# Moving loads ahead of stores at the start of the last part, a limit on how early operations begin, and joined final stores, in an attention + MoE kernel

## The chip, the cores and the metric

The kernel runs on one core of one Trainium2 chip. The metric is device time in microseconds (us) of one execution. One execution of the kernel before was profiled; three more were timed. All times of rows are microseconds from the start of the profiled span.

## What is computed

```python
attn_out = _attn_ref(q, k, v)          # 4 x 8 heads x 576 x 64
x = attn_out.transpose(0, 2, 1, 3).reshape(B * S, H * D)   # 2304 x 512
P = exp(x @ w_gate - max)              # 2304 x 8, then 8 rounds of row and column normalising
for e in range(8):
    h = np.maximum(x @ w1[e], 0.0)     # 512 -> 1024
    out += P[:, e:e + 1] * (h @ w2[e]) # 1024 -> 512
```

The attention is a sum of a coarse attention (over averages of four rows) and a local one. The last part, which the change is about, holds only MoE work: `h`, `h @ w2`, the gates and the sum over the experts, for the last third of the rows.

## The kernel before

Matrix products are made in fp32 precision out of three passes: each operand is split into a high part (`hi`, rounded, on ACT) and a low part (`lo`, the rest, on POOL or DVE), and hi·hi, hi·lo and lo·hi are added in PSUM. One product of a 256 x 512 block therefore is 6 matmuls of 512 columns.

The rows are cut in six chunks. The attention runs first, with MoE work of early chunks beside it; then comes a part in plain tiles and in blocks for chunks 0 to 3 (`blocks_part`, `plain_part` from line 2537); the **last part** (class `Plan`, `final_plan` at line 171, class `Final`) does chunks 4 and 5, `side_c` and `side_d`, for all 8 experts. It uses seven block products in the place of eight (the additions of blocks are on POOL for the weights and on DVE for the results). There are 16 steps, one for each expert and half of the hidden layer. A step has 14 products of the first layer (`l1`, matmuls of line 478, parts a and b) and 14 of the second (`l2`, line 490), 168 matmuls in all. A step's second layer runs between the products of the next step's first layer (`MID`); the first step begins with a first layer alone (`PRO`: a1 a2 a6 a5 b1 b2 a7 a4 a3 b6 b5 b7 b4 b3), and the last ends with `TAIL`, which also transposes the four sums back (`x11`, `x22`, `x12`, `x21`, line 528), copies them out of PSUM (line 537 on DVE, line 497 on ACT) and stores them (`x_store`, line 539).

The order of the last part's instructions on each engine is written by a list scheduler, `Plan.schedule` (line 95). Each operation has a cost and a due time, counted back from the matmuls that need it; each engine in turn takes, of what is ready, the operation with the earliest due time, as early as its inputs and buffers allow. The result is `work`, a list in the order of planned starts. The engines execute their own instructions strictly in that order, so an instruction that waits holds up all that stand behind it on the same engine.

The operations that matter here are:

- Weight loads (`w_load`, lines 440 and 445), issued by SP. A step has four blocks of 256 KB for each layer. First-layer blocks (ring `r1`, 7 buffers; they appear as `xh` and `xl`) take two DMAs of 128 KB, second-layer blocks (ring `r2`, 7 buffers, `r` and `r2x`) one. `r2x` is the seventh buffer of `r2` and lies in the pool `accc`, in memory that is free only after `few.close()`, when the sums of the part before have been stored.
- Gate loads (`g_load`, line 467; `ring g`, 3 buffers): 256 KB that spread one expert's gates over all partitions. Their buffers were used before by `t_gen`, whose last operations are those of line 2397.
- Conversions of weights: `hi` on ACT (line 457), `lo` on POOL (line 461), sums of blocks on POOL (line 448). Copies of PSUM into SBUF on ACT (line 497, `s`, `u`).

The last part begins inside the part before. `plain_part` has 8 steps, numbered -8 to -1 in `ahead`. At steps -3, -2 and -1 the operations are emitted whose planned start lies before the step's end; all others follow after the last step:

```python
            if i >= -3:
                while work and work[0].start < lead + (i + 1) * period_:
                    work.pop(0).emit()
```

In step -1, ahead of this, `closed` (line 2342) stores the four finished tiles of chunks 1 and 2: 16 DMAs of 64 KB on SP (line 2346), which wait for DVE's last sums (line 2363). By the plan, the four first-layer loads of the first step and the first gate load stand before these stores; the second gate load, all second-layer loads and the loads of the second step stand behind them.

At the end, `x_store` stores each of the eight 128 x 512 result tiles with four DMAs of 64 KB, all on SP: 32 in all.

Of the kernel before, what the change touches and what calls it, by code (L numbers as in the profile page):

```python
# [18 lines left out]
HOP_US = 0.06  # L19


class Op:
    def __init__(self, name, eng, iss, lat, deps, port, emit):
        self.name, self.eng, self.iss, self.lat, self.deps = name, eng, iss, lat, deps
        self.port, self.emit, self.users, self.vals, self.due = port, emit, [], [], None
        self.start = self.end = None
# [10 lines left out]
class Plan:  # L37
# [54 lines left out]
    def dma(self, name, kb, reads, writes, emit=None):  # L92
        return self.op(name, "sp", kb / 190.0, 2.2 + kb / 190.0, reads, writes, emit)

    def schedule(self, begin=None):
        begin = begin or {}
        t = begin.get("pe", 0.0)
        for o in self.seq:
            o.due = t
            t += o.iss  # L100
        for a, b in zip(self.seq, self.seq[1:]):
            if a not in b.deps:
                b.deps.append(a)
        vals = {}
        for o in self.ops:
            for v in o.vals:
                vals[id(v)] = v
        for v in vals.values():
            for o in v.new if v.before else ():
                o.deps += [d for d in v.before.all if d not in o.deps]  # L110
        for o in self.ops:
            for d in o.deps:
                d.users.append(o)
        left, topo = {id(o): len(o.deps) for o in self.ops}, [o for o in self.ops if not o.deps]
        for o in topo:
            for u in o.users:
                left[id(u)] -= 1
                if not left[id(u)]:
                    topo.append(u)
        assert len(topo) == len(self.ops)  # L120
        for o in reversed(topo):
            if o.eng != "pe":
                o.due = min(
                    [u.due - (o.iss if u.eng == o.eng else o.lat + HOP_US) for u in o.users], default=t + 1.0
                )
        clk = {e: begin.get(e, 0.0) for e in ("pe", "dve", "act", "pool", "sp")}
        clk["port"] = 0.0
        left = {id(o): len(o.deps) for o in self.ops}
        ready = {e: [] for e in clk}
        at = {}  # L130

        def release(o):
            at[id(o)] = max(
                [d.start + d.iss if d.eng == o.eng else d.end + HOP_US for d in o.deps], default=0.0
            )
            ready[o.eng].append(o)

        for o in self.ops:
            if not o.deps:
                release(o)  # L140
        done = []
        while len(done) < len(self.ops):
            best = None
            for e, l in ready.items():
                if not l:
                    continue
                z = [(max(at[id(o)], clk[e], clk["port"] if o.port else 0.0), o) for o in l]
                m = min(q[0] for q in z) + 0.05
                st, o = min((q for q in z if q[0] <= m), key=lambda q: q[1].due)
                if best is None or st < best[0]:  # L150
                    best = st, o
            st, o = best
            o.start, o.end = st, st + o.lat
            clk[o.eng] = st + o.iss
            if o.port:
                clk["port"] = st + o.iss
            ready[o.eng].remove(o)
            done.append(o)
            for u in o.users:
                left[id(u)] -= 1  # L160
                if not left[id(u)]:
                    release(u)
        return done
# [173 lines left out]
class Final:  # L337
# [1 line left out]

    TYPES = ("B11", "B21", "B22", "T1", "T2", "T3", "T4")  # L340

    def __init__(self, nc, pools, dram, x01, x, xt, sides, xq, w1, w2, lg, tbase, ident, out_rows):
        self.nc, self.pools, self.x01, self.xt, self.sides, self.xq = nc, pools, x01, xt, sides, xq
        self.lg, self.tbase, self.ident, self.out_rows = lg, tbase, ident, out_rows
        self.gd = dram.tile([8, 8, 128], F32, name="gd")
        self.w1 = w1.rearrange("e (k p) (h a i c) -> e p h i a k c", p=128, h=2, a=2, i=2)
        self.w2 = w2.rearrange("e (h a k p) (i c) -> e p h k i a c", p=128, h=2, a=2, i=2)
        self.made = {}
        (ah, bh_), (al, bl_) = ([z[c] for c in sides] for z in x)
        top, bot = slice(0, 2), slice(2, 4)  # L350
        self.x_op = {"B11": (ah[:, top], al[:, top]), "B21": (ah[:, bot], al[:, bot]), "B22": (bh_[:, bot], bl_[:, bot])}
        for i in range(4):
            s = slice(2 * i, 2 * i + 2)
            self.x_op[f"T{i + 1}"] = xt[0][:, s], xt[1][:, s]
        self.b_top = [z[:, k] for z in (bh_, bl_) for k in range(2)]
        self.pages_h = None
# [181 lines left out]

    def x_store(self, blk, j, o):
        i, c = int(blk[0]) - 1, self.sides[int(blk[1]) - 1]  # L540
        t_ = self.get(o[0])
        for t in range(2):
            for p0, m, dst in self.out_rows(c, 2 * j + t):
                self.nc.sync.dma_start(
                    out=dst[:, 256 * i:256 * i + 256], in_=t_[p0:p0 + m, 256 * t:256 * t + 256]
                )


@with_exitstack
def attention_moe_kernel(  # L550
# [10 lines left out]
    nc = tc.nc  # L561
# [4 lines left out]
    R = 4  # L566
# [11 lines left out]
    chunks = [(64 * i, 64) for i in range(3)] + [(192 + 128 * i, 128) for i in range(3)]  # L578
    NC = len(chunks)
    ntile = [R * n // 128 for _, n in chunks]  # L580
    tbase = [sum(ntile[:c]) for c in range(NC)]
# [11 lines left out]
    dram = ctx.enter_context(tc.tile_pool(name="dram", bufs=1, space=bass.MemoryType.DRAM))  # L593
# [9 lines left out]
    ident = const.tile([128, 128], F32, name="ident")  # L603
    lg = const.tile([128, NTILE, E], F32, name="lg")
# [4 lines left out]
    xh, xl = [None] * NC, [None] * NC  # L609
    xq_of = []  # L610
    x01 = []
# [31 lines left out]
    def mask_of(c):  # L643
        i = edged.index(c)
        return mask[:, i * 2 * R * W:(i + 1) * 2 * R * W]
# [65 lines left out]
    class Slot:  # L711
        def __init__(self):
            self.busy = False
            self.t = 0.0
# [1387 lines left out]
    def out_rows(c, t):  # L2102
# [3 lines left out]
        k_ = 128 // m  # L2106
        return [(m * i, m, rows[k_ * t + i, t0 // 2:t0 // 2 + m, :]) for i in range(k_)]

    with tc.manual_schedule():

        ini_ctx = ExitStack()
# [42 lines left out]
        for big in (True, False):  # L2154
            if big:
                fold(64)
            else:
                for o in (32, 96):
                    nc.vector.tensor_scalar(
                        out=eff[o:o + 32], in0=eff[o:o + 32], scalar1=-float(WR * 32), scalar2=None, op0=ALU.add  # L2160
                    )
            for c in edged:
                if is_small(c) == big:
                    continue
                t0, n = chunks[c]
# [4 lines left out]
                dst = mask_of(c)  # L2170
                nc.vector.tensor_scalar(
                    out=dst, in0=eff, scalar1=z + 0.5, scalar2=NEG, op0=ALU.is_le, op1=ALU.mult
                )
                nc.vector.scalar_tensor_tensor(
                    out=dst, in0=eff, scalar=a - 0.5, in1=dst, op0=ALU.is_ge, op1=ALU.mult
# [57 lines left out]
        begin = {"pe": 36.6, "dve": 38.2, "act": 39.0, "pool": 42.3, "port": 38.2, "sp": 42.0, "dma": 48.0}  # L2233
# [39 lines left out]
        n = m_end[0] // NF * NF  # L2273
# [5 lines left out]
        side_f, side_b, side_c, side_d = (1, 2), (3,), (4,), (5,)  # L2279
# [38 lines left out]
        th4 = cx.tile([128, 2 * KD, NS * 2], F32R, name="th4")  # L2318
        tl4 = cx.tile([128, 2 * KD, NS * 2], F32R, name="tl4")
# [447 lines left out]
        if both:  # L2767
# [10 lines left out]
            blocks_part(side_f, side_b, both, hf_a, hf_b, accp, g1, plain1, reload)  # L2778
        final = Final(
            nc, dict(wa=wa, wb=wb, ct=ct, hp=hp, rawp=rawp, ps_h=ps_h, ps_a=ps_a, ps_y=ps_y, ps_z=ps_z), dram,  # L2780
            x01, (xh, xl), (th4, tl4), (side_c[0], side_d[0]), xq_of[0], moe_w1, moe_w2, lg, tbase, ident, out_rows,
        )
        plan = final_plan(E * NH, final)
        lead = 12.0
        work = plan.schedule({"pe": lead})
        period_ = 5.45

        def ahead(i):
            if i == -8:
                final.gates()  # L2790
            if i >= -3:
                while work and work[0].start < lead + (i + 1) * period_:
                    work.pop(0).emit()

        plain_part(rest2, n + n1, len(units), t_gen(side_c, side_d, True), ahead)
        while nb[1] < len(back):
            back_add()
# [35 lines left out]
```

## Time and profile before

| | us |
|---|---|
| profiled execution | 1611.02 |
| its span (first to last instruction) | 1609.2 |
| three timed runs | 1611.98, 1614.25, 1614.31 (median 1614.25) |

The span holds all but 1.8 us of the profiled execution. In the slices, each digit is the busy share of a fortieth of the span in tenths; PEclk is the granted TensorE clock. In the timeline, a row is start, duration, engine, line and operation; in brackets stands the idle time of the engine ahead of it and what ended it. SPq and ACTq are the sequencers that issue DMAs.

### The profile page before, as it was taken

The numbers are of one execution on the slowest core, as the hardware profiler recorded it, in microseconds if no ns is written. First come the engines' busy times: TensorE is split into PE (matmuls) and PEld (weight loads), VectorE is DVE, ScalarE is ACT, GpSimd is POOL, SyncE is SP. The second block draws the span as 40 slices with busy tenths as digits, with TensorE's granted clock in tenths as the row PEclk, the third lists the DMA queues.
The fourth block names the chain that finished last, engine by engine and source line by source line (L and its number), as shares of the span: only waits on it lengthen the run. The fifth ranks groups of instructions, "written<-read, shape, count | busy, mean of one in ns | idle before, by whom it ended". The sixth has DMA issues, their size and how long they took to land.

```text
span 1609.2 us, 23207 instructions
## 1 busy us (share of the span) xinstructions
PE 1573.5 (98%) x7776; PEld 1308.5 (81%) x7776; DVE 1269.2 (79%) x1694; ACT 766.1 (48%) x1625; POOL 1018.9 (63%) x932
## 2 busy tenths in 40 slices
PE   9999999999999999999999997999999999999996
PEld 7888888888888788888888875788888888888885
DVE  8779998878888696477444465989999999999995
ACT  4553555465545443333333334555555555555542
POOL 6698666868495300455544245887888788887760
PEclk9999999999999999999999998999999999999998
DMA  8877767868684545354111433212222212121102
GB/s 202 212 212 208 166 164 183 209 184 220 146 230 125 154 141 178 90 152 118 53 52 50 127 90 102 72 53 73 63 75 58 80 54 66 53 66 53 46 14 53
DMA packets 224454, 186.96 MB, mean 116 GB/s; under 512 B 26126, under 2 KB 181966, under 8 KB 224078
## 3 DMA queue, kind: packets, MB, share of 16 engines
q1 hardware_dynamic: 218382, 174.72, 40.2%
q10 hardware_dynamic: 5952, 10.75, 1.9%
q8 instruction: 61, 1.00, 0.3%
q14 instruction: 59, 0.48, 0.1%
HBM read 165.33 MB, written 20.09 MB: 115 GB/s over the span
## 4 chain that ended last, share of the span: by engine, by line
PE 88%; DVE 5%; DMA 2%; SPq 2%; POOL 1%; issue 1%; ACT 1%; ACTq 0%; POOLq 0%; DVEq 0%
PE psm L490 17%; PE psm L478 17%; PE psh L1847 16%; PE psm L2596 7%; PE psy L1875 5%; PE psy L1876 5%; PE psy L1877 5%; PE psy L2678 3%; PE psy L2676 3%; PE psy L2677 3%; PE psh L2078 1%; DMA r<-in_moe_w_dram 1%; SPq L841 1%; DVE psm L500 1%; PE pss L1472 1%
## 5 line engine op out<-in xcount | busy, mean ns | idle before, releaser
L1996 POOL TENSOR_TENSOR w1l<-r,w1h 128x512 fp32r<-128x512 f32 x112 | 158.1, 1412 | 81.9 <-ACT w1h L1973 73.1
L478 PE MATMUL psm<-th,o 128*128 128x512 f32 x512 | 174.6, 392 | 13.1 <-ACT s L497 13.1
L1996 POOL TENSOR_TENSOR w2l<-r,w2h 128x512 fp32r<-128x512 f32 x114 | 155.6, 1365 | 28.7 <-ACT w2h L1973 28.4
L1875 PE MATMUL psy<-w2h,hh 128*128 128x512 f32 x416 | 168.6, 405 | 0.0
L1876 PE MATMUL psy<-w2l,hh 128*128 128x512 f32 x416 | 162.6, 391 | 0.0
L1877 PE MATMUL psy<-w2h,hl 128*128 128x512 f32 x416 | 162.5, 391 | 0.0
L461 POOL TENSOR_TENSOR o<-r,o 128x512 fp32r<-128x512 f32 x84 | 114.4, 1362 | 75.1 <-ACT o L457 59.9
L500 DVE TENSOR_TENSOR acc<-psm,acc 128x512 f32<-128x512 f32 x216 | 143.7, 681 | 18.3 <-PE psm L490 18.2
L490 PE MATMUL psm<-hx,o 128*128 128x512 f32 x576 | 154.4, 390 | 0.6 <-DVE hx L515 0.6
L1904 ACT ACTIVATE hh<-psh 128x512 fp32r<-128x512 f32 (+1 forms) x136 | 67.5, 496 | 159.9 <-PE psh L1847 151.3
L461 POOL TENSOR_TENSOR o<-xh,o 128x256 fp32r<-128x256 f32 x132 | 107.7, 821 | 42.8 <-ACT o L457 42.5
L2433 POOL TENSOR_TENSOR c1l<-r,c1h 128x512 fp32r<-128x512 f32 (+1 forms) x48 | 58.6, 1248 | 119.4 <-ACT c1h L2430 119.4
L478 PE MATMUL psm<-xh,o 128*128 128x512 f32 x384 | 131.3, 390 | 1.9 <-DVE hx L515 1.9
L1907 DVE SCALAR_TENSOR_TENSOR hl<-psh,hh 128x512 fp32r<-128x512 f32 (+1 forms) x136 | 76.3, 561 | 70.2 <-ACT hh L1904 70.0
L490 PEld LDWEIGHTS psm<-hx,o 128*128 128x128 f32 x576 | 108.0, 188 | 23.4 <-DVE hx L515 1.0
L1973 ACT ACTIVATE w2h<-r 128x512 fp32r<-128x512 f32 x133 | 83.7, 629 | 89.3 <-PE psy L1877 25.5
L478 PEld LDWEIGHTS psm<-th,o 128*128 128x128 f32 x512 | 96.9, 189 | 34.5 <-ACT s L497 14.4
L1847 PE MATMUL psh<-xhs,w1h 128*128 128x256 f32 (+1 forms) x384 | 124.7, 325 | 0.3 <-ACT xhs L1613 0.3
L1847 PE MATMUL psh<-xhs,w1l 128*128 128x256 f32 (+1 forms) x384 | 122.5, 319 | 1.5 <-DVE w1l L1992 1.5
L1847 PE MATMUL psh<-xls,w1h 128*128 128x256 f32 (+1 forms) x384 | 122.3, 319 | 0.2
L1058 DVE TENSOR_REDUCE lo<-prod 128x256 f32<-128x1792 f32 x32 | 109.5, 3423 | 0.4
L478 PE MATMUL psm<-tl,o 128*128 128x512 f32 x256 | 100.3, 392 | 0.0
(329 smaller groups left out, 4417.7 us busy)
## 6 DMA issues: line engine op xcount, KB each, us to landing
r<-in_moe_w_dram SPq DMA_DIRECT2D x391, 256.0 KB
spill<-sp ACTq DMA_DIRECT2D x40, 256.0 KB
s<-spill SPq DMA_DIRECT2D x40, 256.0 KB
xh<-in_moe_w_dram SPq DMA_DIRECT2D x76, 128.0 KB
xl<-in_moe_w_dram SPq DMA_DIRECT2D x52, 128.0 KB
g<-gd SPq DMA_DIRECT2D x16, 256.0 KB
sums<-dr SPq DMA_DIRECT2D x36, 64.0 KB
r2x<-in_moe_w_dram SPq DMA_DIRECT2D x9, 256.0 KB
```

The lines of the kernel that those rows point to most:

```text
L461: (self.nc.gpsimd if pool else self.nc.vector).tensor_tensor(out=o["l"], in0=self.w_view(l, r, ps), in1=o["h"].bitcast(F32), op=ALU.subtract)
L478: self.nc.tensor.matmul(out=ps, lhsT=wt[:, k], rhs=xt[:, k], start=start and n == 0, stop=n == 5, skip_group_check=not start,)
L490: self.nc.tensor.matmul(out=ps, lhsT=wt[:, a, 128 * m:128 * m + 128], rhs=ht, start=start and n == 0, stop=n == 5, skip_group_check=not start,
L500: self.nc.vector.tensor_tensor(out=self.get(o[0]), in0=self.get(a[0]), in1=self.get(b[0]), op=op)
L1058: nc.vector.tensor_reduce(out=ot[:, :, h % 2], in_=pr.rearrange("p r w d -> p r d w"), axis=AX.X, op=ALU.add,)
L1847: nc.tensor.matmul(out=ps, lhsT=w[:, kk], rhs=x[:, kk], start=(kk == 0 and j == 0), stop=(kk == 3 and j == 2),)
L1875: nc.tensor.matmul(out=ye[z], lhsT=hh[:, ts], rhs=h2, start=(f2 == 0), stop=False)
L1876: nc.tensor.matmul(out=ye[z], lhsT=hh[:, ts], rhs=l2, start=False, stop=False)
L1877: nc.tensor.matmul(out=ye[z], lhsT=hl[:, ts], rhs=h2, start=False, stop=(f2 == NF - 1))
L1973: nc.scalar.activation(out=h, in_=r, func=AF.Copy)
L1996: nc.gpsimd.tensor_tensor(out=l, in0=r, in1=h.bitcast(F32), op=ALU.subtract)
L2596: nc.tensor.matmul(out=ps, lhsT=wt[:, kk], rhs=xt[:, kk], start=start and j == 0, stop=j == len(seq) - 1, skip_group_check=not start,)
```

## The change

Three edits. In `schedule`, an operation that is on neither PE nor SP may not begin earlier than its due time less 18 us. In `ahead`, at step -2, all loads that depend on nothing, but for the one into `r2x`, are emitted at once, and so ahead of the stores of step -1. In `x_store`, a DMA takes the rows of two 128-row tiles in place of one (`out_pair` in place of `out_rows`), so that a result tile takes two DMAs of 128 KB; the first is issued by SP, the second by ACT.

```diff
-    def schedule(self, begin=None):
+    def schedule(self, begin=None, ahead=1e9):
...
             at[id(o)] = max(
-                [d.start + d.iss if d.eng == o.eng else d.end + HOP_US for d in o.deps], default=0.0
+                [0.0 if o.eng in ("pe", "sp") else o.due - ahead]
+                + [d.start + d.iss if d.eng == o.eng else d.end + HOP_US for d in o.deps]
             )
...
-        t_ = self.get(o[0])
-        for t in range(2):
-            for p0, m, dst in self.out_rows(c, 2 * j + t):
-                self.nc.sync.dma_start(
-                    out=dst[:, 256 * i:256 * i + 256], in_=t_[p0:p0 + m, 256 * t:256 * t + 256]
-                )
+        v = self.get(o[0]).rearrange("p (t d) -> p t d", t=2)
+        for n, (p0, m, dst) in enumerate(self.out_pair(c, 2 * j)):
+            (self.nc.scalar if n else self.nc.sync).dma_start(
+                out=dst[:, :, 256 * i:256 * i + 256], in_=v[p0:p0 + m]
+            )
...
+    def out_pair(c, t):
+        t0, n = chunks[c]
+        m = n // 2
+        rows = out.rearrange("(t r) d -> r t d", r=2 * R)
+        k_ = 128 // m
+        return [
+            (m * i, m, rows[k_ * t + i:k_ * (t + 1) + i + 1:k_, t0 // 2:t0 // 2 + m, :].rearrange("r t d -> t r d"))
+            for i in range(k_)
+        ]
...
-        work = plan.schedule({"pe": lead})
+        work = plan.schedule({"pe": lead}, 18.0)
...
+            if i == -2:
+                for o in [o for o in work if o.eng == "sp" and not o.deps and (o.vals[0].ring, o.vals[0].i) != ("r2", 6)]:
+                    work.remove(o)
+                    o.emit()
             if i >= -3:
```

## Rows read from the trace of the kernel before

**Rows 1.** The page: busy tenths of TensorE and its granted clock in 40 slices.
```profile
PE   9999999999999999999999997999999999999996
PEclk9999999999999999999999998999999999999998
```

**Rows 2.** Windows: start:end, length, busy time of each engine, PEclk, DMA share, GB/s.
```profile
960.00:970.00 10.00, 4.03 (x18) 3.00 (x16) 2.10 (x4) 1.54 (x5) 6.52 (x9) 0.96 0.45 116
970.00:980.00 10.00, 4.25 (x11) 3.40 (x12) 1.39 (x2) 3.64 (x8) 3.50 (x5) 0.53 0.89 254
...
1100.00:1200.00 100.00, 100.00 (x443) 82.84 (x442) 94.10 (x138) 55.97 (x115) 78.88 (x79) 1.00 0.21 59
```

**Rows 3.** Timeline of PE at the start of the last part.
```profile
963.64 0.39 PE L478 MATMUL psm<-xh,o 128*128 128x512 f32 x1
975.75 0.80 PE L478 MATMUL psm<-th,o 128*128 128x512 f32 x1 [11.71 <-ACT s L497]
...
980.26 0.39 PE L478 MATMUL psm<-xh,o 128*128 128x512 f32 x1
...
1013.93 0.50 PE L478 MATMUL psm<-xh,o 128*128 128x512 f32 x1 [1.86 <-DVE hx L515]
```

**Rows 4.** Timeline of ACT in the same stretch.
```profile
962.44 0.42 ACT L457 ACTIVATE o<-xh 128x256 fp32r<-128x256 f32 x1 [0.97 <-POOL xh L448]
974.58 0.63 ACT L457 ACTIVATE o<-r 128x512 fp32r<-128x512 f32 x1 [11.72 <-DMA r<-in_moe_w_dram]
975.11 0.58 ACT L497 ACTIVATE s<-psm 128x512 f32<-128x512 f32 x1
```

**Rows 5.** Timeline of the SP queue: DMA issues.
```profile
952.42 0.37 SPq L467 DMA_DIRECT2D g<-gd  x1
960.09 7.41 SPq L2346 DMA_DIRECT2D out_dram<-acc  x16
967.60 0.39 SPq L467 DMA_DIRECT2D g<-gd  x1
968.08 0.47 SPq L445 DMA_DIRECT2D r<-in_moe_w_dram  x1
...
976.28 8.43 SPq L440 DMA_DIRECT2D xh<-in_moe_w_dram  x6
```

**Rows 6.** Waits of the SP queue, 930 to 1025 us: total, times, longest.
```profile
SPq L467 <- DVE tl L2397: 17.0, 1, 17.0
...
SPq L445 <- DMA g<-gd: 1.8, 1, 1.8
```

**Rows 7.** Windows of one us, as in Rows 2: a gate load alone, then weight loads.
```profile
954.00:955.00 1.00, 1.00 (x6) 0.84 (x5) 0.19 (x1) 0.00 (x0) 0.00 (x0) 1.00 0.37 86
...
974.00:975.00 1.00, 0.00 (x0) 0.00 (x0) 0.00 (x0) 0.42 (x1) 0.00 (x0) 0.50 1.12 357
```

**Rows 8.** Timeline of DVE: the last users of the gate buffers.
```profile
951.71 2.49 DVE L2397 TENSOR_TENSOR tl<-bsum,th 128x512 fp32r<-128x512 f32 x4
```

**Rows 9.** Timeline of ACT: the second step's first converted late load, and what follows.
```profile
988.57 0.41 ACT L457 ACTIVATE o<-xh 128x256 fp32r<-128x256 f32 x1
989.86 0.60 ACT L497 ACTIVATE u<-psm 128x512 f32<-128x512 f32 x1 [0.89 <-DVE psm L500]
```

**Rows 10.** Timeline of the end: SP queue and ACT's last copies.
```profile
1596.80 10.12 SPq L544 DMA_DIRECT2D out_dram<-xl  x16
...
1594.81 0.60 ACT L497 ACTIVATE xl<-psm 128x512 f32<-128x512 f32 x1 [3.02 <-PE psm L528]
1596.47 0.60 ACT L497 ACTIVATE xl<-psm 128x512 f32<-128x512 f32 x1 [1.06 <-PE psm L528]
```

**Rows 11.** Instructions by tile: DMA issues, ns min/median/max, first and last start.
```profile
L544 SPq DMA_DIRECT2D out_dram<-xl x16: 540/594/596, 1596.8 to 1606.3; - x16
...
L1949 ACTq DMA_DIRECT2D spill<-sp x40: 326/327/439, 86.9 to 545.3; - x40
```

**Rows 12.** Window at the end, as in Rows 2.
```profile
1602.00:1604.00 2.00, 0.00 (x0) 0.00 (x0) 0.00 (x0) 0.00 (x0) 0.00 (x0) 0.50 0.45 108
```

More of the change, by code (lines that the diff above doesn't have):

```diff
@@ L340, with __init__ @@
     TYPES = ("B11", "B21", "B22", "T1", "T2", "T3", "T4")
-    def __init__(self, nc, pools, dram, x01, x, xt, sides, xq, w1, w2, lg, tbase, ident, out_rows):
+    def __init__(self, nc, pools, dram, x01, x, xt, sides, xq, w1, w2, lg, tbase, ident, out_pair):
         self.nc, self.pools, self.x01, self.xt, self.sides, self.xq = nc, pools, x01, xt, sides, xq
-        self.lg, self.tbase, self.ident, self.out_rows = lg, tbase, ident, out_rows
+        self.lg, self.tbase, self.ident, self.out_pair = lg, tbase, ident, out_pair
         self.gd = dram.tile([8, 8, 128], F32, name="gd")
@@ L2780, in attention_moe_kernel @@
             nc, dict(wa=wa, wb=wb, ct=ct, hp=hp, rawp=rawp, ps_h=ps_h, ps_a=ps_a, ps_y=ps_y, ps_z=ps_z), dram,
-            x01, (xh, xl), (th4, tl4), (side_c[0], side_d[0]), xq_of[0], moe_w1, moe_w2, lg, tbase, ident, out_rows,
+            x01, (xh, xl), (th4, tl4), (side_c[0], side_d[0]), xq_of[0], moe_w1, moe_w2, lg, tbase, ident, out_pair,
         )
```

## The prediction, made before the changed kernel ran

> **What bounds the kernel now.** I began with the slices of the page. TensorE is busy in all 40, but for one digit 7, which also has the lower clock, and a 6 in the last [rows 1]. So nearly everything is TensorE's own work, and whatever can be won lies at two places. The windows narrow the first one: between 960 and 980 us TensorE works 4.03 and 4.25 of 10 us each, and in the second ten the granted clock is 0.53, half of full speed; later, from 1100 to 1200 us, it works 100 of 100 us at full clock with 443 matmuls, 0.226 us each, while DVE has 94.10 and POOL 78.88 [rows 2]. The second place is the end, where the last work of an engine, ACT's copy, ends at 1597.07 us (1596.47 + 0.60) and the span runs on to 1609.2 us: 12.1 us of stores alone [rows 10].
>
> The timelines say what the first wait is. TensorE's last matmul before it starts at 963.64 us, the next at 975.75 us, after 11.71 us of waiting for ACT's copy `s` [rows 3]. ACT was free at 962.86 us (962.44 + 0.42); it did not copy, since the conversion of a second-layer block `r` stands ahead of the copy in its order, and that waited 11.72 us for its load [rows 4]. The load was late because SP issued it at 968.08 us, behind 16 stores that take the queue from 960.09 to 967.5 us, and those had to wait for the sums [rows 5]. So the chain is stores, load, conversion, copy, matmul. Nothing needs this load before the second layer begins; it only stands in front of something urgent. After the wait the 12 matmuls from 975.75 to 980.26 us take 4.51 us [rows 3]; at 0.226 us each they would take 2.71. The clock had fallen to its lower level while TensorE stood still.
>
> **Loads ahead of the stores.** At step -2 ten more loads are emitted before the stores: the second gate, four of the second step's and of the second layer's blocks, and so on; in DMAs, twelve from the first gate on (3 gates, 5 `r`, 2 `xl` blocks of two DMAs each). SP can issue none of them before 952.42 us, as the first gate waited 17.0 us for line 2397 [rows 5, 6]. That line's last four operations run from 951.71 to 954.20 us and free the buffers one by one [rows 8]; the second gate needs the third, about 953.6 us, so `r` is issued near 954.1 us. The data come in order: a gate of 256 KB moves alone at 86 GB/s with the DMA engines 0.37 busy, about 3.1 us, while weight loads go at 357 GB/s, about 0.8 us for 256 KB [rows 7]. The first gate, issued at 952.42 us, is through near 956.5 us; the second near 959.6; `r` lands near 961. ACT wants it at 962.86 us. So the wait goes, with some 2 us in hand. Then conversion 0.63 and copy 0.58 [rows 4] put the copy's end near 964.1 us, 0.1 behind the last matmul: I count **-11.5 us**. Without the long pause the clock has no reason to fall: **-1.8 us** (4.51 - 2.71). POOL was 6.52 us busy from 960 to 970 [rows 2], so it kept working during part of the wait and will be some 2.5 us further behind TensorE than before; I cost that at nothing, since its next results are needed several products later; without that cover it costs up to those 2.5 us, which I keep for the range.
>
> What is late next? SP's queue. A ninth DMA seems to wait for the first one still out: the second of three `r` behind the gate waited 1.8 us for that gate's data [rows 6]. So of the twelve, the last, a gate, goes out near 962 us and moves until about 968 us behind the other data, at its slow rate. The stores follow: some go out from 962 us on, the rest only after that gate, at 0.46 us each (7.41 / 16, [rows 5]), until about 973 us. Behind the stores stand `r2x`, whose memory may have to wait for one of them, and the second step's first `xh` loads. Those were issued from 976.28 us [rows 5]; now it is 974.5 to 976 us, with landing some 2.5 us later, 977 to 978.5 us (an estimate from the last store, whose start lies 2.9 us before the end of the span [rows 11]). But TensorE is 13.3 us earlier: the conversion of that block, 988.57 us, moves to 975.3 us, and behind it on ACT stands the copy `u`, 989.86 us [rows 9], wanted at 976.6 us, which a product of TensorE waits for. That is a new wait of the old kind, 0 to 3 us; from below, nothing lets it turn into a gain. I take **+1.3 us**.
>
> **The limit of 18 us.** By the planner's own list only 32 of ACT's 692 operations, 91 of POOL's 480 and 15 of DVE's 820 were planned more than 18 us ahead of need, most of them POOL's sums of weight blocks, so few instructions change place. In the first step, one helps: the second `r` conversion moves behind ACT's copy `u` of part a. In the 100 us window TensorE never waits [rows 2], so there is nothing to win there: **0**, bounds -1 and +3 us (POOL bunching up, DVE order near the one remaining wait of 1.86 us [rows 3]); the cover is POOL's idle 21 of 100 us. I take 0, since the rows nearest to it show slack.
>
> **The final stores.** Before, the last 16 issues begin at 1596.80 us and take 10.12 us, 0.63 each; the last starts at 1606.3 us [rows 10, 11], and the span ends 2.9 us after it. Copying has long finished: issuing is the bound, as the DMA engines are only 0.45 busy at 108 GB/s [rows 12]. After, 16 DMAs are left, half of them on ACT. ACT copies the last tile until 1597.07 us (in the old clock), with one of its stores already issued after the copy that ends at 1595.41 us; three remain, starting near 1597.1, 1597.7 and 1598.3 us if an issue of 128 KB costs what one of 64 KB does. SP is done before that. With 2.9 us behind the last start and 0.3 us for the larger block, the span would end at 1601.5 us: **-7.7 us**. The cost of the new issue is not in the trace. The cheapest is ACT's for the spill, 0.33 us, the dearest twice the present, 1.19 us for twice the rows [rows 11]. The first gives -8.2 us; the second delays ACT's last copy by 0.2 us and gives -6.4 us. I take the nearest row, the same pattern at 64 KB.
>
> Here a page of the Trainium skill speaks against the edit. "DMA: Bandwidth & Descriptors", section "Issuing engines are not separate DMA queues", says that issuing from several engines saves only the sequencers' issue time, which is usually small beside the transfer. In this tail the trace has it the other way, issue 10.12 us for 1 MB with engines 0.45 busy, so the measurement decides; what the rule would give is the second rival.
>
> **Sum:** -11.5 - 1.8 + 1.3 + 0 - 7.7 = **-19.7 us** against the profiled execution's 1611.0 us: 1591.3 us. The median of the runs shown is 3.2 us above that execution; by it, 1594.5 us. I predict 1593 us, between the two. A difference of 0.2%, 3.2 us, is about what a measurement of this kernel can tell from none.
>
> **Rivals.**
> 1. *The wait moves to the second step.* The queue of 28 DMAs in front of `r2x` and the `xh` loads clears late, or the gates hold back the first `r`, and TensorE loses 4 to 7 us more than I count, with a clock drop if it is one long pause. For: gates at a third of the engines' rate, three of them now ahead of everything. Against: 2 us in hand for `r`. It gives 1597 to 1600 us. Chance 0.16.
> 2. *The tail is bound by data.* If 108 GB/s is the stores' own rate, the last 1 MB (eight DMAs of 128 KB from about 1596 us) takes 9.7 us, to 1605.7. Of the 2.9 us behind the last start, 0.6 are issue and 0.6 the transfer of 64 KB at that rate, so 1.7 follow: 1607.4 us, 1.8 us saved in place of 7.7. Sum -13.8: 1597 to 1600.5 us. Against: the engines' share of 0.45. Chance 0.05.
> 3. *Slower: the limit starves TensorE.* If POOL's block sums, now planned up to 19 us later, push POOL's low parts behind TensorE in each step, the loss repeats about 15 times. It outweighs the gain by 0.2% from (19.7 + 3.2) / 15 = 1.5 us a step on; at 2 us a step the time is about 1623 us. For: POOL at 78.88 and DVE at 94.10 of 100. Against: few operations move and 21 us of 100 are free on POOL. Chance 0.03.
> 4. *The loads are not early.* Something ahead of them, such as a buffer that is freed later than I read, holds SP until the stores. Then only the tail gains: about 1605 us. Chance 0.04.
>
> **The numbers.** The forecast has 0.72: 17 to 23 us of gain, 1588 to 1597 us by either base. The range of 1588 to 1600 us takes in rivals 1 and 2 in most cases. Faster by over 0.2%: 0.96 (all but rival 3 and a remainder), within 0.2%: 0.01, slower: 0.03.
>
> **What will show it.** Right: the 16 stores of line 2346 stand behind the `r` issues; no wait of ACT for `r` above 1 us near 963 us; the granted clock at 1.0 from 960 to 980 us; TensorE's last transposes about 12 us earlier; 16 issues of line 544, half from ACT, and the span ending 4 to 5 us after ACT's last copy. The place to watch is ACT's conversion of the second step's `xh` near 975 us: a wait for a DMA there is my +1.3 us. I am wrong if TensorE has repeated gaps from 1020 to 1560 us, if the first `r` lands after 965 us, or if the last DMA engines are fully busy while the issues are over.

## The result, and the profile after

The changed kernel takes 1592.41 us in the median (4 runs, 1592.2 to 1593.41), the kernel before 1614.28 us on the same chip (4 runs, 1611.98 to 1614.82). The ratio is 0.9868, interval 0.9851 to 0.9886: 1.3% faster. Forecast were 1593 us and 1588 to 1600. The profiled execution took 1592.54 us, its span 1590.8 us, against 1609.2 before: 18.4 us less.

The page of the changed kernel: busy time of the engines, then the slices of TensorE and its clock.

```profile
PE 1572.3 (99%) x7776; PEld 1307.2 (82%) x7776; DVE 1250.8 (79%) x1694; ACT 764.1 (48%) x1625; POOL 1009.7 (63%) x932
...
PE   9999999999999999999999999999999999999998
PEclk9999999999999999999999999999999999999999
```

The 7 of [rows 1] is gone, and the last digit is 8 in place of 6. The windows of the changed kernel, columns as in [rows 2]:

```profile
960.00:970.00 10.00, 9.71 (x43) 7.56 (x42) 4.32 (x7) 6.45 (x17) 10.00 (x13) 1.00 0.87 269
970.00:980.00 10.00, 8.88 (x37) 6.38 (x35) 9.06 (x13) 5.58 (x12) 9.92 (x11) 1.00 0.66 183
...
1020.00:1060.00 40.00, 38.52 (x169) 31.38 (x169) 35.73 (x52) 21.19 (x46) 32.56 (x33) 1.00 0.26 67
1100.00:1200.00 100.00, 100.00 (x443) 82.81 (x442) 88.27 (x135) 54.16 (x113) 76.19 (x79) 1.00 0.27 74
...
1587.00:1588.00 1.00, 0.00 (x0) 0.00 (x0) 0.00 (x0) 0.00 (x0) 0.00 (x0) 0.82 0.98 294
```

From 960 to 980 us TensorE works 18.6 of 20 us, where it worked 8.3, with the granted clock at 1.00. The steady stretch is as it was, 443 matmuls in 100 us. But from 1020 to 1060 TensorE falls 1.5 us short, and its timeline names the place, the last line here:

```profile
964.29 0.50 PE L479 MATMUL psm<-th,o 128*128 128x512 f32 x1 [0.29 <-ACT s L498]
...
972.17 0.50 PE L479 MATMUL psm<-th,o 128*128 128x512 f32 x1 [0.69 <-ACT s L498]
...
980.41 0.51 PE L479 MATMUL psm<-th,o 128*128 128x512 f32 x1 [0.83 <-ACT s L498]
...
1001.34 0.50 PE L479 MATMUL psm<-xh,o 128*128 128x512 f32 x1 [1.86 <-DVE hx L516]
...
1037.70 0.50 PE L491 MATMUL psm<-xhs,o 128*128 128x512 f32 x1 [1.48 <-DVE o L462]
```

The first line answers to the wait of 11.71 us in [rows 3]; 0.29 is left of it. The 1.86 us at 1001.34 is the old wait of 1013.93 us. The 1.48 us at 1037.70 is new: TensorE waits for DVE's conversion of a second-layer weight block, for which it waited 0.12 us in the kernel before. ACT's timeline shows how the first wait went:

```profile
963.12 0.63 ACT L458 ACTIVATE o<-r 128x512 fp32r<-128x512 f32 x1 [0.29 <-DMA r<-in_moe_w_dram]
963.66 0.58 ACT L498 ACTIVATE s<-psm 128x512 f32<-128x512 f32 x1
...
976.53 0.42 ACT L458 ACTIVATE o<-xh 128x256 fp32r<-128x256 f32 x1
977.27 0.60 ACT L498 ACTIVATE u<-psm 128x512 f32<-128x512 f32 x1 [0.32 <-DVE psm L501]
...
1585.21 0.60 ACT L498 ACTIVATE xl<-psm 128x512 f32<-128x512 f32 x1 [1.00 <-PE psm L529]
1585.27 2.04 ACTq L544 DMA_DIRECT2D out_dram<-xl  x3
```

And the SP queue's:

```profile
952.38 0.97 SPq L468 DMA_DIRECT2D g<-gd  x2
953.45 0.46 SPq L446 DMA_DIRECT2D r<-in_moe_w_dram  x1
...
963.63 0.41 SPq L468 DMA_DIRECT2D g<-gd  x1
964.13 8.92 SPq L2356 DMA_DIRECT2D out_dram<-acc  x16
973.10 0.43 SPq L446 DMA_DIRECT2D r2x<-in_moe_w_dram  x1
973.64 3.14 SPq L441 DMA_DIRECT2D xh<-in_moe_w_dram  x6
...
1584.05 2.78 SPq L544 DMA_DIRECT2D out_dram<-xl  x4
```

The load `r` goes out at 953.45 us in place of 968.08 [rows 5], the 16 stores after it. At the end half of the issues are ACT's. ACT's last copy ends at 1585.81 us (1585.21 + 0.60), and the span 4.99 us later, where it was 12.13.

Two lengths are used from here on, each within one profile. The *part* runs from the first matmul of the last part (961.15 us before, 961.12 after) to the end of ACT's last copy: 635.92 us before, 624.69 after, -11.23. The *tail* runs from there to the end of the span: -7.14. They make the 18.4 us.

### The profile page after: what moved, and what is told of

Its sections match the earlier page's. It is cut to its first block, busy times and chain, and to the rows that moved or that the text cites. A ratio compares the mean times of both kernels' runs of the same rounds, so it can differ in the third digit from the quotient of the medians.

```text
span 1590.8 us, 23162 instructions
## 1 busy us (share of the span) xinstructions
PE 1572.3 (99%) x7776; PEld 1307.2 (82%) x7776; DVE 1250.8 (79%) x1694; ACT 764.1 (48%) x1625; POOL 1009.7 (63%) x932
## 4 chain that ended last, share of the span: by engine, by line
PE 93%; DVE 4%; DMA 1%; SPq 1%; ACT 1%; issue 0%; DVEq 0%; ACTq 0%
PE psh L1847 18%; PE psm L491 18%; PE psm L479 17%; PE psm L2606 7%; PE psy L1875 6%; PE psy L1876 6%; PE psy L1877 6%; PE psy L2688 3%; PE psy L2687 3%; PE psy L2686 3%; PE psh L2078 1%; PE pss L1472 1%; DVE psm L501 1%; DMA xl<-in_moe_w_dram 1%; PE psg L1652 1%; PE psx L1596 0%
```

## The experiments

Diffs are against the changed kernel. Ratios are to the kernel before, whose median was 1613.17, 1613.72 and 1614.43 us on the three chips used: the first four runs on one, the next four on another, the last four on the third. A ratio compares runs round by round, so it isn't quite the quotient of two medians.

**The loads alone** (no limit, the old final stores).

```diff
-        work = plan.schedule({"pe": lead}, 18.0)
+        work = plan.schedule({"pe": lead})
...
-        for n, (p0, m, dst) in enumerate(self.out_pair(c, 2 * j)):
+        for t in range(2):
+            for p0, m, dst in self.out_rows(c, 2 * j + t):
```

> Loads ahead of the stores alone, no limit, old final stores. My theory: nearly the whole gain at the start of the last part comes from this edit, so the time is 10 to 12.5 us below the kernel before (ACT's wait for the first second-layer block from 11.7 to under 0.5 us, clock at 1.0 from 960 to 980 us). Rival, the limit matters: without it the early conversions of ACT stand in front of the copies again, and at least 3 us of the gain are missing (gain under 9 us).

1600.59 us (1598.09 to 1606.79), ratio 0.9936 (0.9919 to 0.9953). Part 624.94 us, tail 12.28: the part is as short as in the changed kernel, the tail as long as before. In this profile TensorE did not wait for DVE's conversion (0.12 us), but its clock fell near 1000 us (last section); both come back in the account below.

**The limit alone** (no block at step -2, the old final stores).

```diff
-            if i == -2:
-                for o in [o for o in work if o.eng == "sp" and not o.deps and (o.vals[0].ring, o.vals[0].i) != ("r2", 6)]:
-                    work.remove(o)
-                    o.emit()
```

> The limit of 18 us alone. My theory: within 1.5 us of the kernel before; TensorE still waits 11 to 12 us for the late load, since the first conversion stands ahead of the copy in this order too. Rival: by moving the conversion behind the copy the limit alone removes the wait, gain 5 us or more. Second rival: it costs TensorE time in later steps (slower by 1.5 us or more, gaps after 1020 us).

1613.99 us, ratio 1.001 (0.9999 to 1.0021). Part 637.79, tail 12.34. From TensorE's timeline and its waits (total, times, longest):

```profile
977.86 0.80 PE L479 MATMUL psm<-th,o 128*128 128x512 f32 x1 [12.01 <-ACT s L498]
...
PE psm L491 <- DVE o L462: 1.5, 1, 1.5
```

The old wait stays, and the new one, for DVE's conversion, is there without any load having moved. That conversion ends 74.7 us after this first matmul (it starts at 1051.89 and takes 0.69), 73.0 us in the kernel before: the limit alone makes it 1.7 us later. It brings no gain, and the part is 1.9 us longer.

**The stores alone** (no block at step -2, no limit).

```diff
-        work = plan.schedule({"pe": lead}, 18.0)
+        work = plan.schedule({"pe": lead})
...
-            if i == -2:
```

> Joined final stores on two queues alone. My theory: 6.5 to 8 us below the kernel before, all of it behind ACT's last copy (12.1 us become about 5). Rival, the tail is bound by data: under 3 us.

1604.17 us, ratio 0.9948 (0.9936 to 0.996). Part 635.86, tail 4.72. The first wait stays, at 11.97 us.

**Loads and stores, no limit.**

```diff
-        work = plan.schedule({"pe": lead}, 18.0)
+        work = plan.schedule({"pe": lead})
```

> The whole change without the limit. If the limit does nothing, within 1 us of the changed kernel and the wait of 1.48 us for DVE's low part near 1037 us is still there. Rival: the limit's new order of POOL and DVE makes that wait and DVE's shorter operations; then without it the wait is gone or DVE's busy time is back at about 1269 us (1251 in the changed kernel), and the time differs by 1 to 2 us.

1592.34 us (1591.18 to 1597.11), ratio 0.9879 (0.9865 to 0.9893), which overlaps that of the whole change. Part 624.78, tail 4.70. The wait for DVE's conversion is gone (0.12 us), and DVE's busy time is back at 1269.6 us: the two signs that the expectation gave for its rival, that the limit's order makes this wait. The difference of 1 to 2 us in time did not come with them. ACT now waits for the second step's `xh`, and TensorE for ACT's copy `u`. From the timelines of ACT and TensorE:

```profile
979.08 0.42 ACT L458 ACTIVATE o<-xh 128x256 fp32r<-128x256 f32 x1 [1.36 <-DMA xh<-in_moe_w_dram]
...
980.03 0.50 PE L479 MATMUL psm<-th,o 128*128 128x512 f32 x1 [1.11 <-ACT u L498]
```

The four runs split the gain: loads about 11 us, stores about 7.3, limit nothing that the times show. What the limit's nothing is made of stands in the account below.

**Joined stores, all issued by SP.**

```diff
-            (self.nc.scalar if n else self.nc.sync).dma_start(
+            self.nc.sync.dma_start(
```

> The changed kernel with the joined stores all on SP. If issuing still bounds the tail, eight issues of 0.6 us stand behind the copy of the third block on one queue in place of four on two: the last starts about 1.8 us later and the span ends 1.0 to 1.8 us later than the changed kernel's. If the tail is now bound by data (DMA engines 0.95 to 0.98 busy from 1586 to 1589 us), the difference is under 0.5 us.

1595.79 us (1594.4 to 1608.32), ratio 0.9905 (0.9874 to 0.9936). Part 624.71, tail 6.42. Timeline of the SP queue and a window near the end:

```profile
1584.67 5.62 SPq L544 DMA_DIRECT2D out_dram<-xl  x8
...
1588.00:1589.00 1.00, 0.00 (x0) 0.00 (x0) 0.00 (x0) 0.00 (x0) 0.00 (x0) 0.50 0.86 199
```

Joining is worth 5.7 us of tail (12.13 - 6.42), the second queue 1.4 more (6.42 - 4.99).

**Single stores on two queues** (32 DMAs of 64 KB, alternating SP and ACT).

```diff
-        for n, (p0, m, dst) in enumerate(self.out_pair(c, 2 * j)):
+        for t in range(2):
+            for n, (p0, m, dst) in enumerate(self.out_rows(c, 2 * j + t)):
```

> The changed kernel with 32 single-tile stores, half on SP and half on ACT. Issue-bound: about as many issues per queue as with joined stores on one queue, plus ACT's last copy held by up to 0.6 us by issues ahead of it: 1.2 to 2.5 us above the changed kernel. Bound by data: under 0.5 us above.

1597.04 us, ratio 0.9895 (0.9878 to 0.9912). Tail 5.82, part 626.81. Two queues without joining win 6.3 us of tail, joining without a second queue 5.7: the two edits take the same thing, issue time, and the second to come finds little left. Both intervals overlap that of the whole change, so the order of the three rests on the tails. The part is 2.1 us longer here. Most of this is a dip of TensorE's clock near 1000 us (last section): 18 matmuls there take 5.84 us, in the changed kernel 4.21. Of the expected 1.2 to 2.5 us above the changed kernel, the tail has 0.83 (5.82 - 4.99).

**DVE's weight conversion moved to POOL.** In each step one block's low half was DVE's; this is the operation of the 1.48 us wait.

```diff
-        plan = final_plan(E * NH, final)
+        plan = final_plan(E * NH, final, dvelo={1: (), 2: ()})
```

> The changed kernel with DVE's one weight conversion per step on POOL (one DVE operation of 0.68 us less and one POOL operation of 1.3 us more per step). If DVE's backlog from the first steps is what gave 1.5 us back at 1037 us, that wait is gone and the time falls by 0.5 to 2 us. Rival: POOL, with 1.3 us more per step, becomes late instead and the time rises by 1 us or more.

1590.83 us (1589.67 to 1596.06), ratio 0.9862 (0.9844 to 0.988). Part 621.06, tail 4.99. The same window as above:

```profile
1020.00:1060.00 40.00, 40.00 (x179) 33.10 (x178) 34.97 (x52) 22.32 (x45) 34.42 (x34) 1.00 0.24 67
```

The wait is gone and TensorE does 179 matmuls where it did 169. So DVE's conversion, not a load, was the last wait of this stretch. The part is 3.6 us shorter: 1.15 us in the first 150 matmuls, 1.78 around the conversion, most of the rest near the end.

**Few loads ahead.** Only loads due within the first 40 us go ahead of the stores, no limit, so that stores end sooner.

```diff
-                for o in [o for o in work if o.eng == "sp" and not o.deps and (o.vals[0].ring, o.vals[0].i) != ("r2", 6)]:
+                for o in [o for o in work if o.eng == "sp" and not o.deps and o.due < 40.0]:
```

> No limit, and only the loads due in the first 40 us of the plan go ahead of the stores, so the third gate and one second-layer block stay behind them. If SP's queue is what holds the second step's first load, the stores end 2 to 4 us sooner, ACT no longer waits for that load (1.36 us without the limit and with all loads ahead) and TensorE not for the copy behind it (1.1 us); the time is 0.5 to 1.5 us below the run with loads and stores without the limit. Rival: the load is held by its buffer and nothing changes.

1596.7 us, ratio 0.9905 (0.9884 to 0.9926). Part 625.95: the expectation fell. Timelines of the SP queue, ACT and TensorE:

```profile
973.01 0.41 SPq L468 DMA_DIRECT2D g<-gd  x1
973.53 3.26 SPq L441 DMA_DIRECT2D xh<-in_moe_w_dram  x6
...
980.01 0.42 ACT L458 ACTIVATE o<-xh 128x256 fp32r<-128x256 f32 x1 [2.59 <-DMA xh<-in_moe_w_dram]
...
980.97 0.50 PE L479 MATMUL psm<-th,o 128*128 128x512 f32 x1 [2.16 <-ACT u L498]
```

The stores did end a microsecond sooner, but the third gate now goes out just ahead of the `xh` loads, which are issued as early as in the changed kernel (973.53 against 973.64) and land later. ACT waits 2.59 us, where it did not wait. What the gate cost here was not its own place in the queue but the slow data that it put in front of the next load.

**That gate behind the `xh` loads** (with the conversion on POOL). Loads due after 50 us are put behind the second step's first loads.

```diff
+        slow = [o for o in work if o.eng == "sp" and not o.deps and o.due > 50.0]
+        for o in slow:
+            work.remove(o)
+        n_ = 1 + max(i for i, o in enumerate(work) if o.eng == "sp" and o.start < 30.0)
+        work[n_:n_] = slow
...
-                for o in [o for o in work if o.eng == "sp" and not o.deps and (o.vals[0].ring, o.vals[0].i) != ("r2", 6)]:
+                for o in [o for o in work if o.eng == "sp" and not o.deps and o.due < 50.0]:
```

> The changed kernel with DVE's weight conversion on POOL, and with the three loads that the plan needs only after 60 us (the third gate and two second-layer blocks) issued after the second step's first-layer loads. If the third gate's slow transfer in front of those loads is what makes ACT wait for the first of them, that wait is under 0.2 us, TensorE does not wait for the copy u behind it, and the time is 0.3 to 1.5 us below the same kernel with the three loads ahead (pool_low). Rival, the stores alone hold the queue long enough: the wait stays at 0.4 us or more and the time is equal.

1593.63 us (1589.27 to 1597.77), ratio 0.9872 (0.9854 to 0.989). Part 623.23. Timelines of the SP queue and TensorE:

```profile
978.21 2.96 SPq L441 DMA_DIRECT2D xh<-in_moe_w_dram  x6
983.26 0.47 SPq L468 DMA_DIRECT2D g<-gd  x1
...
1007.75 0.50 PE L479 MATMUL psm<-xh,o 128*128 128x512 f32 x1 [2.24 <-DVE hx L516]
```

The gate is behind, and TensorE's wait for `u` is gone. Yet the part is no shorter than with the conversion on POOL alone (621.06 here above, 623.22 in its repetition below, which has the same wait of 2.24 us for DVE's `hx`). The expected 0.3 to 1.5 us did not come: mending the order of the queue wins nothing that can be seen.

**The same without the limit.**

```diff
-        work = plan.schedule({"pe": lead}, 18.0)
+        work = plan.schedule({"pe": lead})
```

> The same without the limit of 18 us. If the limit itself is worth nothing, within 1 us of the same kernel with it, with DVE's busy time back near 1267 us. Rival, the limit's new order is worth something once the other waits are gone: 1 us or more above it.

1594.65 us, ratio 0.9881 (0.9864 to 0.9898), part 624.04: not apart from the run before it. In its trace TensorE does 1757 matmuls from 1100 to 1500 us, where it does 1766 in the run before it, in the changed kernel and with loads and stores alone. TensorE is busy 399.85 of the 400 us all the same, so these 2 us (9 at 0.226) go in small pieces. So in this pair of traces the limit saves 2 us of the steady stretch when POOL has more to do; the medians, 1.0 us apart, don't show it.

**The changed kernel and the one with the conversion on POOL, again,** as the same two kernels on one chip with more rounds.

> The changed kernel again, on the same chip as the two versions built on it: 1592 to 1594 us. ACT waits 0 to 1 us for the second step's first load, depending on when the 16 stores clear, and TensorE waits for DVE near 1037 us by about 1.5 us less what it has already lost.

> The changed kernel with DVE's weight conversion on POOL again, on the same chip: 1 to 2 us below the changed kernel, without a wait of TensorE between 1020 and 1060 us. If the earlier difference was only that of two chips, it is under 0.5 us here.

1596.19 us (ratio 0.9892, 0.9874 to 0.9909), above the 1592 to 1594 expected, and 1590.25 us (0.985, 0.9836 to 0.9865). The intervals lie apart: the conversion on POOL beats both kernels. The edit itself is not worth the whole 5.9 us. Part and tail together are 629.65 us for the changed kernel (629.68 in its first profile) and 628.23 with the edit (626.05 in its first profile): 1.4 to 3.6 us. In these two profiles the last part began at 964.75 and at 960.17 us, a difference that the edit, which touches only the last part, can't make. Of the 2.2 us between 1.4 and 3.6, 1.6 are the clock: it fell near 1000 us in the second profile with the edit and not in the first.

## Why the prediction was right, step by step

**The wait and the clock: shown.** Forecast -11.5 and -1.8. Measured -11.42 (11.71 to 0.29) and -1.57: from the first of the matmuls shown above to the second are 7.88 us (972.17 - 964.29), 9.45 us for the same work before. The clock stayed at 1.00 when the pause was gone; with the stores alone, the pause is back. What failed is the margin: `r` was to land near 961 us with 2 us in hand. SP issued it a little earlier than I had it (953.45 for 954.1), but the data of two gates and `r` took until 963.1 us. ACT waited 0.29 us for it. My rate for a gate came from one that moved alone; two together with `r` were no faster, and rival 1 was closer than the 2 us said. Rival 4 is out: the loads went from 952.38 us on, when the first buffer came free.

**The new wait behind the stores: right place, size off.** Forecast +1.3 at ACT's conversion of the second step's `xh`. The load went out at 973.64 us (forecast 974.5 to 976), and in this execution the conversion did not wait. TensorE's next step took 0.40 us longer than before (8.24 us from the second to the third matmul above, 7.84 before), 0.29 of it at the matmul that needs `u`. In six other profiles, the repeated changed kernel's among them, TensorE waited 0.17 to 1.17 us for `u`, and 2.16 us where a gate stood directly ahead of the load. Little of that is lost: with loads and stores alone, TensorE waited 1.11 us for `u`, and yet its first 150 matmuls took 40.06 us, in the changed kernel 40.22, which waited for DVE's `acc` later on instead. Of the 2.16 us, 1.07 were left by then. So the term is 0.4 here and at most about 1.5 in the others.

**The limit: 0 forecast, about +1.4 us measured. This is the step that failed.** I took 0, since the rows nearest to the limit showed slack; but these were rows of the steady stretch, and the cost came in the second step, at the wait of 1.48 us for DVE's conversion. That wait is not what TensorE pays for coming 12 us earlier. It is 1.46 to 1.49 us in all five profiles with the limit and this conversion on DVE, and 0.12 us (less than the timeline names) in all five without the limit, with the loads moved or not. With the limit alone TensorE comes 13 us later than in the changed kernel and waits as long; with single stores on two queues it had lost 1.9 us more by then, and it waited 1.49 us:

```profile
1042.02 0.50 PE L491 MATMUL psm<-xhs,o 128*128 128x512 f32 x1 [1.49 <-DVE o L462]
```

A comparison at equal matmuls shows what the times hid. The table has the time that TensorE takes for the same matmuls of the last part, from their starts in each trace, in us:

| kernel | limit | loads moved | 1st to 150th | 151st to 168th | 301st to 310th |
|---|---|---|---|---|---|
| before | no | no | 52.78 | 4.22 | 2.69 |
| limit alone | yes | no | 53.34 | 4.21 | 4.05 |
| loads alone | no | yes | 40.23 | 5.81 | 2.69 |
| loads and stores | no | yes | 40.06 | 5.84 | 2.69 |
| changed | yes | yes | 40.22 | 4.21 | 4.05 |
| single stores, two queues | yes | yes | 40.46 | 5.84 | 4.06 |
| conversion on POOL | yes | yes | 39.07 | 4.21 | 2.27 |

The 301st to 310th are those around the conversion, the 151st to 168th those behind the wait for `hx`, where the clock fell in some executions. The limit costs 1.36 us at the conversion (4.05 - 2.69). The kernels of the table with the loads moved and without the limit did not pay this, but lost 1.6 us to the clock in their profiles. So parts of 624.7 to 624.9 us came out of three kernels (loads alone, loads and stores, the whole change) by coincidence, and the one with single stores paid both.

In the 20 us ahead of the conversion DVE does the same operations in the same order, but with the limit two of them last longer, and two others swap their lengths. From the timelines of DVE and POOL, with loads and stores and without the limit:

```profile
1019.86 0.70 DVE L516 TENSOR_TENSOR xhs<-m22a,xhs 128x512 fp32r<-128x512 f32 x1
1019.96 1.75 POOL L449 TENSOR_TENSOR r<-r,r2x 128x512 f32<-128x512 f32 x1
...
1025.12 0.68 DVE L507 SCALAR_TENSOR_TENSOR xl<-xl,g 128x512 f32<-128x512 f32 x1
```

And in the changed kernel:

```profile
1017.02 1.29 POOL L449 TENSOR_TENSOR r<-r,r2x 128x512 f32<-128x512 f32 x1
1017.26 1.61 DVE L516 TENSOR_TENSOR xhs<-m22a,xhs 128x512 fp32r<-128x512 f32 x1
...
1022.98 1.28 POOL L449 TENSOR_TENSOR r<-r2x,r 128x512 f32<-128x512 f32 x1
1023.43 1.38 DVE L507 SCALAR_TENSOR_TENSOR xl<-xl,g 128x512 f32<-128x512 f32 x1
```

Where DVE's addition begins first it takes 0.70 us and POOL's sum 1.75; where POOL's begins first it takes 1.29 us and DVE's 1.61. The two operations are 0.91 and 0.70 us longer, 1.6 us together, against the 1.36 us that TensorE loses. That the limit makes the wait is shown; that POOL's place beside DVE is the reason is argued from these overlaps. Moving the conversion to POOL takes the wait away all the same. The cost lies within the bounds of -1 and +3 us, and DVE's order was named there. Rival 3 is out: TensorE has no waits in the steady stretch. POOL's lag, costed at nothing, held: no wait of TensorE in the last part names POOL.

**The tail: -7.7 forecast, -7.14 measured.** The disputed price was the issue of a joined store. Instructions by tile, changed kernel, columns as in [rows 11]:

```profile
L544 SPq DMA_DIRECT2D out_dram<-xl x4: 595/596/647, 1584.1 to 1586.2; - x4
L544 ACTq DMA_DIRECT2D out_dram<-xl x4: 602/624/637, 1584.1 to 1586.7; - x4
```

An issue of 128 KB costs about what one of 64 KB did (0.594 us), 0.596 us on SP and 0.624 on ACT, as I took it. The last issue starts at 1586.7 us; from there to the end are 4.1 us, not the 3.2 I had; its 0.3 us for the larger block rested on no row. The engines are 0.98 busy at 294 GB/s in the window at 1587, as the last issue ends, where before it was 0.45 and 108 [rows 12]. So the last sign of being wrong came true in part: a grain of rival 2, though at nearly three times the rate that it assumed. (The dearest issue would have given -6.3 us by the numbers there, not -6.4.)

That also places the rule that the prediction weighed. The Trainium skill ("DMA: Bandwidth & Descriptors", "Issuing engines are not separate DMA queues") says that a second issuer saves only the time of issuing, usually small beside the DMA. Here a second queue alone saved 6.3 us where issues were the bound, and 1.4 us once joining had halved their number and the engines were nearly full: the trace disagrees in the first case and agrees in the second.

**The sum.** In the part, -11.42 - 1.57 + 0.40 + 1.36 make the -11.23 us, where -12.0 were forecast: a term of +1.3 that came to 0.4 and one of 0 that came to 1.4 nearly cancel, and that is luck. With the tail, the profiles give -18.4 us for -19.7; the medians give -21.9. The profiled execution of before lay 3.2 us below the median of its runs, that of after on its median, so the forecast between the two bases met the median. That it did so within 1 us is luck too.

## What to carry to other kernels

Before an edit is called worth nothing because two times are equal, compare the kernels stretch by stretch at equal numbers of matmuls, as here a cost of 1.4 us and a dip of the clock of 1.6 us hid each other. When an edit changes the order of operations, ask in the stretch with the least slack which of them will now run side by side, and not only how many move. In a queue, look at what the load ahead of the urgent one does to the data, not only at when the urgent one is issued. For a tail of stores, divide its length by the number of issues first: if that gives the issue time, fewer or spread issues help until the DMA engines are full.

## What was not expected

**The limit cut DVE's busy time by 18.8 us, and POOL's by 8, at equal work.** From the page with loads and stores, without the limit:

```profile
PE 1573.7 (99%) x7776; PEld 1308.3 (82%) x7776; DVE 1269.6 (80%) x1694; ACT 766.2 (48%) x1625; POOL 1017.8 (64%) x932
```

The changed kernel has DVE 1250.8 with the same 1694 instructions. From 1100 to 1500 us DVE's additions `xls<-mt,xls` last 1.73 us in the median without the limit (11 of them) and 0.69 us with it (10), while `xls<-m11b,xls` go from 1.23 to 1.78. So the duration of an addition is not fixed by its operands and size alone. The Trainium skill ("SBUF — State Buffer", "Who interferes with whom") says that a DVE instruction with two SBUF inputs contends with a GpSimd instruction that reads SBUF. The durations here, and the overlaps of 1.61 and 1.75 us above, agree with that, but no run changed POOL's neighbour of one such addition alone. Nothing was gained, as DVE was not the bound there; in the second step, where it was, the limit made DVE slower.

**Short waits and the clock.** After the waits of about 2 us near 1000 us the granted clock fell in some executions and not in others (the changed kernel: 1.00 after 1.86 us). The window of the run with the loads alone:

```profile
1000.00:1005.00 5.00, 3.99 (x11) 3.13 (x12) 3.90 (x5) 2.43 (x6) 3.81 (x4) 0.66 0.04 8
```

Where it fell, TensorE lost about 1.6 us. It did so in six of the eleven profiles with the loads moved and in none of the three without, and of two profiles of the kernel with the conversion on POOL in one. What decides it is open.

**The start of the last part moves.** It began between 960.2 and 968.2 us in the profiles, in kernels that hardly differ before it. That is more than most effects studied here, so lengths within a profile tell them apart better than the times.
